# Second half of the key images transposed on TensorE instead of by DMA, with the order of the work searched anew

## The chip, the core and the metric

The kernel runs on one core of one Trainium2 chip. The metric is the device time of one execution in microseconds (us); the lower, the better. The profiles in this document each show one execution, and the times are medians of several executions.

## What is computed

Two kinds of layer alternate, twice each, over x of 2048 tokens by 512 features: x = x + A(layernorm(x)), x = x + B(layernorm(x)), and the same again. The cut reference of A, with 32 heads of 128 features, 8 memory rows and segments of 32 tokens:

```python
for s in range(n_seg):                      # 64 segments, one after the other
    h = concatenate([mem, xs[s]])           # 8 memory rows + 32 tokens = 40 rows
    q, k, v = h @ Wq, h @ Wk, h @ Wv        # each [32 heads, 40, 128]
    p = softmax(where(mask, q @ k.T * scale, -1e9))
    o = (p @ v, all heads) @ Wo             # [40, 512]
    mem = o[:8]                             # the next segment needs this
    outs.append(o[8:])
```

B is linear attention without a mask: phi(q) times the sum of phi(k) v over all tokens, divided by phi(q) times the sum of phi(k), times wo. Inputs and output are bfloat16.

## The kernel before, in words

The 64 segments of an A layer depend on each other through the memory rows, so the kernel goes through 2 x 64 steps in sequence. In step s the stationary operand of TensorE is `hT`, the 32 columns (8 memory rows and the first 24 tokens of the segment) of the current block; the last 8 tokens of four segments make up a "left" block of their own, which is prepared ahead for a group G of four segments (`prepare`, `left_block`). A step consists of these parts, named here by their place in the plan:

- `k0`, `k1`, `q0`, `q1` (function `turned`): `project` multiplies the block by half of a weight matrix (b = 0 or 1). It does so in 16 matmuls (L794), each with 512 moving columns: four chunks of the features, and for each chunk one matmul on each of the array's four 32-column strips. The result is evacuated by ACT or DVE (L623 or L624) into an `img` buffer, 128 x 512 in bfloat16. This image has to be transposed in blocks before attention can use it. There are two ways, chosen by the argument `dma`: one DMA transpose issued from SP (L807) that writes `kT` or `qT` directly, or 16 matmuls against the identity (L816) into a PSUM tile and one more evacuation of 128 x 512.
- `v0`, `v1`: the same projection, evacuated without a transpose.
- `mem0`, `mem1` (`mem_attention`, one call for each half b): scores against the left keys (L943, 4 matmuls) and against `kT` (L937, 16 matmuls), exp on ACT (L954), weights on DVE (L964), column sums on TensorE (L970), ln and exp on ACT (L973, L975), weighted values on TensorE (L980, L983), and the product on DVE (L987).
- `out`: the output projection (L1085, 64 matmuls of 256 columns on 32-column strips), and two evacuations into `outW`.
- `next` (`next_mem`): the new memory rows are moved into place by small matmuls (L1110), then evacuated into the next `hT`. The projections of step s + 1 start from there.
- `x` (`x_attention`, L1019, L1015, L1051, L1055): attention of the 24 tokens, which only the next step's `out` needs. Left blocks, layernorms (`prep`, L765), residual rows and B's work for finished tiles (`bi`, `bo`, L1247, L1281, L1350, L1358) lie between these parts too.

Before the change both halves of the keys go by DMA in all steps but the first and the last of a layer (62 steps in each of two layers, so 248 DMA transposes); the queries always go over TensorE. The left blocks use DMA transposes too (232 of them, L807, L829, L875). All of them are issued by SP, in one queue.

The order of the work is not written by hand. Every operation is a node of a planner (`_Prog`). `schedule` assigns nodes to engines and fixes each engine's order when the program is built, with costs such as 0.17 us + 0.833 ns per element for ACT, and for a key's DMA transpose a time to landing of `TURN` + 0.2 = 2.0 us. Among ready nodes the highest priority goes first: minus (step x `PERIOD` + `OFFSET` of the place). `OFFSET` is a table of several hundred numbers, found by a search. `MODE_SLACK` says how much priority TensorE gives up to stay in the same mode ("col" for 32-column strips, "full" for the whole array), and `LOOK` how long TensorE may be left waiting for a more urgent node. The engines then execute these fixed orders with semaphore waits: an instruction that waits holds up all that stands behind it on its engine.

Of the kernel before, what the change touches and what calls it, by code (L numbers as in the profile page):

```python
# [16 lines left out]
HOP = 0.06  # L17
PE_SWITCH = 0.1
TURN = 1.8
MODE_SLACK = 192.230600  # L20

LOOK = 0.053000

PERIOD = 13.5
OFFSET = {
# [2 lines left out]
    "ld2": (0.00,),  # L28
    "ld3": (0.00,),
    "ld4": (0.00,),  # L30
    "startF": (-170.65,),
    "prepF": (-362.95, -276.40, -279.35, -312.25, -284.40, -217.25, -201.70, -91.90, -249.05, -348.60, -91.55),
    "left0F": (-416.25, -385.35, -190.40, -192.15, -191.50, -260.05, -185.05, -323.65, 49.05, -312.35, -318.60,
        -241.55, -302.65, -428.10),
    "left1F": (-193.15, -172.40, -166.05, 8.55, -258.70, 143.10, -33.70, -147.70, -290.10, -305.35, 95.80, -299.95,
        -122.50, -62.05),
    "leftv0F": (-428.45, -202.00, -272.00, -246.25, -281.55, 122.35, -299.95, -328.60, -403.90),
    "leftv1F": (-236.20, -263.35, -302.50, -297.40, -85.80, -45.90, 124.65, 2.20, -49.90),
    "leftsF": (-234.20, -375.85, -265.20, -250.15),
    "xlF": (-310.30,),  # L40
    "k0F": (-347.90, -327.85, -45.95, -130.00, -426.00, -164.90, -319.75),
    "k1F": (-399.90, -270.75, -170.05, -162.00, -401.55, -54.25, -374.20),
    "q0F": (-283.40, -269.55, -303.95, -408.95, -255.55, 69.25, -299.55),
    "q1F": (-204.75, -132.60, -288.35, -54.15, -258.85, -365.30, -182.50),
    "v0F": (-414.65, -223.40, -19.35, 81.75, -230.45),
    "v1F": (-401.65, -20.40, -368.15, -227.30, 51.20),
    "qlF": (-245.40, -114.85),
    "mem0F": (-317.25, -11.55, -397.30, -321.65, -320.25, -248.15, -253.70, -229.35, -133.00, -179.30),
    "mem1F": (-370.65, -140.65, -279.95, -318.75, -212.15, -221.80, -405.65, -341.75, -281.65, -211.10),
    "warm": (42.25,),  # L50
    "outF": (-402.35, -81.30, -402.15, -242.85, -347.15, -401.55, -307.80, -298.10, -276.25, -259.15),
    "nextF": (-375.70, -276.25, -244.45),
    "xF": (-98.95, -278.35, -377.95, -152.15, -135.25, 32.50, -346.60, -281.05, -333.80, -305.40, -12.30, -315.60,
        -254.25, -391.50, -398.50, -375.10, -142.10, -246.05, -334.30, -87.65, -255.15, -235.40, 13532.05),
    "k0": (-401.55, -410.00, -408.65, -395.35, -74.20, -387.80),
    "k1": (-391.95, -393.55, -385.95, -421.75, -30.10, -383.50),
    "q0": (-390.25, -317.80, -318.55, -319.05, -274.20, -209.45, -235.60),
    "q1": (-318.10, -268.15, -290.55, -290.35, -195.95, -199.55, -227.60),
    "v0": (48.50, -288.20, -280.75, -292.45, -407.80),
    "v1": (-129.55, -240.70, 55.90, -105.15, -237.95),  # L60
    "ql": (-280.90, -136.95),
    "mem0": (-26.85, -405.55, -408.25, -272.75, -279.50, -104.85, -278.45, -267.70, -46.10, -243.25),
    "mem1": (-310.50, -287.80, -241.60, -278.85, -365.10, -292.95, -265.00, -282.35, -102.40, -283.10),
    "out": (-25.50, -276.55, -294.25, -203.55, -206.65, -210.35, -252.50, -482.00, -293.65, -307.90),
    "next": (-255.55, -256.05, -278.85),
    "res": (236.50, -313.60, -391.85, -316.15, -318.45, -213.15, -208.95, -209.00, -293.25, 28.80, -279.90,
        -138.50, 15.90, -283.25, -219.80),
    "x": (-93.20, -38.25, -293.70, -268.95, -391.70, -282.75, -266.00, -265.05, -145.40, -288.95, -131.60, -62.40,
        -274.15, -533.80, -295.10, -243.65, -187.65, -24.75, -364.70, -413.90, -387.65, -216.80, -254.50),
    "prep": (1.35, -36.30, -223.35, -207.00, -267.90, -50.60, -49.25, -48.35, -273.10, -44.30, -306.65),  # L70
    "left0": (-48.30, -401.20, -399.80, -62.90, -46.25, 32.70, -54.85, -105.00, -281.40, -268.85, -253.85, -280.75,
        -398.85),
    "left1": (-203.20, -273.65, -253.00, -268.75, -275.85, -144.15, -240.85, -222.15, -62.15, -26.20, -324.35,
        -249.50, 164.80),
    "leftv0": (-197.90, -242.35, -154.55, -352.25, -27.40, -18.85, -389.90, -343.05),
    "leftv1": (-37.05, -37.20, -17.30, 77.70, -243.10, -422.10, -312.45, -147.50),
    "lefts": (-233.40, -231.20, -282.65, -281.10),
    "xl": (8.50,),
    "bi": (-193.05, -276.60, -31.20, -282.75, -309.65, -103.40, -411.75, -293.35, -60.50, -323.30, -306.25, -50.60,
        222.00, -26.45, -419.70, 153.25, -239.30, -268.60, -45.00, -406.05, 10.80, 235.95, -34.25, -253.30,  # L80
        -258.15, -283.80, -225.85, -253.40, -289.90, -455.50, -380.70, -330.00),
    "k0L": (-397.65, -321.00, -290.45, -295.10, -149.00, -211.05, -209.60),
    "k1L": (-315.55, -249.05, -284.25, -222.90, -300.80, -226.80, -358.55),
    "lr": (-281.60, -387.40, -223.70, -194.55, -163.65, -294.00, -403.80, -281.80, -54.95, -32.55, -208.50,
        -309.95, -290.45),
    "xL": (-216.70, -398.20, -62.05, -12.50, -5.65, -146.85, -275.80, -37.65, 42.50, -160.75, -241.30, -2.50,
        -431.00, -191.10, -201.00, -409.30, -21.65, -235.10, -274.75, 30.60, -86.15),
    "outL": (-332.60, -340.75, -182.95, -373.55, -30.55, -381.10, -253.00, -312.90, -416.90, -25.90),
    "resL": (-28.25, -281.80),
    "biL": (-252.95, -263.60, -283.55, -413.10, -366.90, -266.00, -247.00, -280.95, -270.35, -405.60, -300.70,  # L90
        136.55, -156.95, -222.15, -94.65, 144.10, -155.20, -300.55, -274.15, -80.30, -106.30, -268.10, -202.50,
        -72.35, -256.40, -293.85, -84.10, -275.70, -178.05, -227.25, 24.00, -302.35),
    "bm": (-260.20, -231.30, -199.90, -417.75, -164.00, -416.45, -315.35, -149.90, -246.65, -188.85, -306.65,
        -193.85, -304.25),
    "boF": (-243.70, -216.35, -419.65, -205.95, -58.65, -230.20, -354.85, -261.35, -168.20, -314.80, -202.35),
    "bo": (-261.70, -389.05, -8.40, -226.30, -208.05, -365.20, 89.15, -317.00, -313.75, -60.60, -263.60),
    "ldL": (-267.05, -251.65),
    "boL": (-188.90, -322.50, -307.65, -221.35, -371.35, -300.60, -211.05, -102.75, -186.05, -221.05),
    "boZ": (-261.45, -73.35, -318.25, -222.40, -39.10, -170.70, -12.60, -83.90, -205.70, -19.35),
}  # L100


# [404 lines left out]
def _build_kernel(nc, A_x, A_mem0, A_Wq, A_Wk, A_Wv, A_Wo, A_seg_len, B_wqkv, B_wo, out):  # L507
# [8 lines left out]
    NSEG = S // SEG  # L516
# [18 lines left out]
    Wk_sb = sb("Wk_sb", [128, 4, H * DH])  # L535
# [45 lines left out]
    kT = av(1024).rearrange("p (h j x) -> p h j x", h=8, j=4)  # L581
# [195 lines left out]
    def a_layer(base, first):  # L777
# [413 lines left out]
        for s in range(NSEG):  # L1191
            G, g = divmod(s, 4)
            r2 = s % 2
            blk = hT[:, G % 2, g, :, :]
            bk = [("hTm", G % 2, g), ("hTx", G % 2, g)]
            if g == 0 and G + 1 < NT:
                tokens(G + 1, s)
            for b in range(2):
                at(s, "k%d" % b)
                turned(Wk_sb, "Wk", blk, bk, b, kT[:, 4 * b:4 * b + 4, :, :], ("kT", b), True, 0 < s < NSEG - 1)  # L1200
            for b in range(2):
                at(s, "q%d" % b)
                turned(Wq_sb, "Wq", blk, bk, b, qT[:, 4 * b:4 * b + 4, :, 0:32], ("qT", b), True, False)
            for b in range(2):
                at(s, "v%d" % b)
                tl = project(Wv_sb, "Wv", blk, bk, b, True)
                evac(vimg[:, r2, 512 * b:512 * b + 512], lambda tl=tl: tl.f32()[:, :], 512, tiles=[tl],
                     writes=[("v", r2, b)], urgent=True)
            for b in range(2):
                mem_attention(s, b)  # L1210
            if first and s == 0:
                warm(0, 14, [n for n in P.nodes if n.key == (0, "mem1F", 1)])
            w_of[s] = out_block(s)
            if s + 1 < NSEG:
                next_mem(s, w_of[s][0])
            if s > 0:
                residual((s - 1) // 4, (s - 1) % 4, w_of[s])
                if g == 0:
                    b_in(base + s + 2, G - 1, not first)
            x_attention(s)  # L1220
            if g == 2 and G + 1 < NT:
                prepare(G + 1, s)
# [197 lines left out]
```

## Time and profile before

| what | value |
|---|---|
| time, median of 3 runs | 1782.08 us (1778.4 to 1785.93) |
| profiled execution, its own time | 1783.98 us |
| span of the profiled execution | 1781.8 us |
| mean granted TensorE clock | 0.991 |
| PE matmul busy | 1656.4 us (93%) |
| PE weight load busy | 1063.9 us (60%) |
| DVE busy | 1062.1 us (60%) |
| ACT busy | 1172.9 us (66%) |
| POOL busy | 326.5 us (18%) |
| DMA transposes issued by SP | 480 |

"Busy" of PE counts a matmul from its start to its modelled end, and matmuls overlap, so it is not the share of PE's peak. "Idle before" and the waits name the instruction whose end released an engine. In the chain of waits, the run is followed back from its last instruction to what released each step.

### The profile page before, as it was taken

Reading aid. Unit: us, or ns where it says so; the run is one execution under the profiler, and the core shown is the slowest. Engines: PE = TensorE matmul, PEld = TensorE weight load, DVE = VectorE, ACT = ScalarE, POOL = GpSimd, SP = SyncE. Lnnn points to the kernel's source line nnn. Section 1 sums busy time; section 2 is a strip of 40 time slices with the busy share of each in tenths; the row PEclk is TensorE's granted clock in tenths of the full one; section 3 lists DMA queues with packets and bytes.
Section 4 is the critical chain, followed back from the end, with each engine's and each line's share of the span. In section 5 each row is a group of like instructions: output and inputs, shape, how many; then the busy total and the mean of one; then the engine's idle time right before and its main releaser. Section 6 shows DMA issues by size and latency. Waiting matters only on the chain.

```text
span 1781.8 us, 96722 instructions
## 1 busy us (share of the span) xinstructions
PE 1656.4 (93%) x43964; PEld 1063.9 (60%) x44043; DVE 1062.1 (60%) x3788; ACT 1172.9 (66%) x3117; POOL 326.5 (18%) x660
## 2 busy tenths in 40 slices
PE   5999999999999999999799999999999999999996
PEld 2656656665666665566456566666666656666563
DVE  3456666665666566565555666666665656665656
ACT  3666666666666666666466677767766766676665
POOL 2011211112121111222102111122221112221120
PEclk9999999999999999999899999999999999999998
DMA  9323323323233332332012333233333333332323
GB/s 378 79 48 53 56 54 51 61 49 56 53 53 57 51 61 44 57 56 50 25 33 42 59 56 60 50 56 59 53 62 56 54 54 54 56 59 53 62 76 99
DMA packets 295978, 113.46 MB, mean 64 GB/s; under 512 B 274552, under 2 KB 289712, under 8 KB 294032
## 3 DMA queue, kind: packets, MB, share of 16 engines
q1 hardware_dynamic: 272240, 74.91, 23.8%
q0 software_dynamic: 21744, 19.78, 5.3%
q10 hardware_dynamic: 1584, 12.58, 1.7%
q8 instruction: 344, 5.64, 1.4%
q14 instruction: 66, 0.54, 0.1%
HBM read 29.63 MB, written 10.49 MB: 23 GB/s over the span
## 4 chain that ended last, share of the span: by engine, by line
PE 62%; DMA 21%; DVE 9%; ACT 5%; issue 2%; POOL 1%; ACTq 0%; DVEq 0%
PE pb L794 31%; DMA arena_sb<-arena_sb 14%; PE pb L1085 11%; PE pb L1247 3%; PE pb L1051 3%; DVE arena_sb L624 3%; DMA dx_sb<-y_sb 2%; DMA arena_sb<-pq_scratch 2%; PE pb L816 2%; PE pb L970 2%; PE pb L937 2%; ACT arena_sb L623 1%; DMA Wk_sb<-in_A_Wk_dram 1%; DMA pq_scratch<-arena_sb 1%; PE pb L1110 1%
## 5 line engine op out<-in xcount | busy, mean ns | idle before, releaser
L623 ACT ACTIVATE arena_sb<-pb 128x512 bf16<-128x512 f32 (+6 forms) x1433 | 710.0, 500 | 295.7 <-PE pb L794 186.9
L639 POOL DMA_DIRECT2D dx_sb<-y_sb x504 | 253.7, 509 | 1126.1 <-DVE arena_sb L624 659.8
L794 PE MATMUL pb<-Wv_sb,arena_sb 128*32 128x512 bf16 x5120 | 357.3, 378 | 2.8 <-issue 2.8
L794 PE MATMUL pb<-Wk_sb,arena_sb 128*32 128x512 bf16 x5120 | 344.5, 383 | 5.0 <-DMA Wk_sb<-in_A_Wk_dram 4.2
L794 PE MATMUL pb<-Wq_sb,arena_sb 128*32 128x512 bf16 x5120 | 345.8, 381 | 0.9 <-DMA Wq_sb<-in_A_Wq_dram 0.6
L1085 PE MATMUL pb<-Wo_sb,arena_sb 128*32 128x256 bf16 x10368 | 335.1, 273 | 7.6 <-DVE arena_sb L987 5.9
L624 DVE COPY arena_sb<-arena_sb 128x128 bf16<-128x128 bf16 (+2 forms) x973 | 207.6, 213 | 148.2 <-DMA arena_sb<-arena_sb 92.6
L1085 PEld LDWEIGHTS pb<-Wo_sb,arena_sb 128*32 128x32 bf16 x10368 | 261.0, 97 | 47.2 <-DVE arena_sb L987 13.7
L624 DVE COPY arena_sb<-pb 128x512 bf16<-128x512 bf16 (+2 forms) x311 | 117.9, 381 | 192.3 <-PE pb L816 171.5
L624 DVE CAST arena_sb<-pb 128x512 bf16<-128x512 f32 (+3 forms) x388 | 186.7, 488 | 43.5 <-PE pb L794 29.5
L794 PEld LDWEIGHTS pb<-Wk_sb,arena_sb 128*32 128x32 bf16 x5120 | 127.6, 97 | 130.7 <-DVE arena_sb L624 18.8
L794 PEld LDWEIGHTS pb<-Wq_sb,arena_sb 128*32 128x32 bf16 x5120 | 134.9, 97 | 114.6 <-issue 2.1
L794 PEld LDWEIGHTS pb<-Wv_sb,arena_sb 128*32 128x32 bf16 x5120 | 113.2, 95 | 59.3 <-issue 4.3
L623 ACT ACTIVATE outW_sb<-pb 128x128 fp32r<-128x128 f32 x290 | 80.5, 278 | 100.8 <-PE pb L1085 90.2
L954 ACT ACTIVATE arena_sb<-pb 128x192 bf16<-128x192 f32 (+1 forms) x256 | 84.1, 328 | 86.1 <-PE pb L937 84.2
L964 DVE TENSOR_TENSOR arena_sb<-arena_sb 128x128 bf16<-128x128 bf16 x504 | 90.6, 221 | 25.9 <-ACT arena_sb L954 22.2
L816 PEld LDWEIGHTS pb<-id_sb,arena_sb 128*32 128x32 bf16 x4320 | 81.6, 97 | 32.0 <-ACT arena_sb L623 1.5
L1051 PE MATMUL pb<-arena_sb 128*128 128x128 bf16 x1024 | 98.5, 220 | 1.8 <-ACT arena_sb L623 0.7
L816 PE MATMUL pb<-id_sb,arena_sb 128*32 128x128 bf16 x4320 | 96.8, 219 | 0.7 <-ACT arena_sb L623 0.7
L987 DVE TENSOR_TENSOR arena_sb<-pb,arena_sb 128x128 bf16<-128x128 f32 x252 | 68.9, 288 | 43.4 <-ACT arena_sb L975 32.3
L937 PE MATMUL pb<-arena_sb 128*32 128x40 bf16 x4096 | 69.2, 180 | 27.2 <-DMA arena_sb<-arena_sb 26.7
L1121 DVE TENSOR_TENSOR y_sb<-pb,outW_sb 64x256 bf16<-64x256 f32 x158 | 65.7, 416 | 41.9 <-ACT outW_sb L623 37.8
(122 smaller groups left out, 1964.5 us busy)
## 6 DMA issues: line engine op xcount, KB each, us to landing
arena_sb<-arena_sb SPq DMA_TRANSPOSE x480, 2.8
Wq_sb<-in_A_Wq_dram ACTq DMA_DIRECT2D x1, 4096.0 KB, 13.8
Wk_sb<-in_A_Wk_dram ACTq DMA_DIRECT2D x1, 4096.0 KB, 24.7
Wv_sb<-in_A_Wv_dram ACTq DMA_DIRECT2D x1, 4096.0 KB, 35.1
Wo_sb<-in_A_Wo_dram SPq DMA_DIRECT2D x4, 1024.0 KB, 11.7
xs_scratch<-x_sb POOLq DMA_DIRECT2D x32, 128.0 KB, 2.1
pq_scratch<-arena_sb POOLq DMA_DIRECT2D x32, 128.0 KB, 2.3
dx_sb<-y_sb POOLq DMA_DIRECT2D x252, 12.0 KB, 2.0
```

Source lines behind the costliest of these rows:

```text
L623: return e.activation(o() if callable(o) else o, i() if callable(i) else i, ACTF.Copy)
L624: return e.tensor_copy(o() if callable(o) else o, i() if callable(i) else i)
L639: add(eng, lambda e: e.dma_start(o, i), 0.55 if eng == "pool" else 0.4, reads=reads, writes=writes, dsem="%s%d" % (kind, k), lat=lat + (0. ...
L794: r = pe.matmul(tl.f32()[32 * j:32 * j + 32, 0:512], blk[:, c, :], W[:, c, o:o + 512], start=(c == 0), stop=(c == 3), tile_position=(0, 32 ...
L816: r = pe.transpose(tt.bf16()[32 * j:32 * j + 32, 128 * i:128 * i + 128], img[:, k, o:o + 32], id_sb[:, :], tile_position=(0, 32 * j))
L937: r = pe.matmul(tl.f32()[32 * j:32 * j + 32, 40 * i:40 * i + 40], kT[:, hh, j, :], qT[:, hh, j, :], start=True, stop=True, tile_position=( ...
L954: add("act", lambda a: a.activation(PQ[:, r2, b, 0:nq], tl.f32()[:, 0:nq], ACTF.Exp, scale=SCALE), c_act(nq), tiles=[tl], writes=[("PQ", r ...
L964: add("dve", lambda v, a=a, p_=p_, w_=w_: v.tensor_tensor(wide(Pm[:, k, a, :]), p_.unsqueeze(2).to_broadcast([128, 4, 4, 8]), w_, ALU.mult ...
L987: add("dve", lambda v: v.tensor_tensor(oTb[:, s % NO, 16 * b:16 * b + 16, 0:8], pv.f32()[:, 0:128].rearrange("p (n q) -> p n q", q=8), Rm[ ...
L1051: r = pe.matmul(o, vimg[:, r2, e], Pbx[:, hh, :, :], start=i == 0, stop=False, skip_group_check=True)
L1085: r = pe.matmul(tl.f32()[32 * j:32 * j + 32, 0:256], oT[:, 4 * hh + n, :], Wo_sb[:, 8 * n + hh, 256 * d:256 * d + 256], start=(hh == 0 and ...
L1121: add("dve", lambda v: v.tensor_tensor(y_sb[0:64, k, :], tl.f32()[0:64, 0:256], outW[64:128, w, :].bitcast(F32), ALU.add), c_dve(256), rea ...
```

## The change

In the steps where both halves of the keys went by DMA, only half b = 0 still does; half b = 1 is transposed on TensorE, by the code that serves the queries. In addition `MODE_SLACK`, `LOOK` and the whole table `OFFSET` are replaced, so the order of the instructions on all engines is another one. The functions are otherwise the same.

```diff
-MODE_SLACK = 192.230600
+MODE_SLACK = 257.520800
-LOOK = 0.053000
+LOOK = 0.037900
 OFFSET = {
...
-    "k1": (-391.95, -393.55, -385.95, -421.75, -30.10, -383.50),
+    "k1": (-365.35, -358.40, -356.75, -359.10, -107.85, -297.25, -150.20),
...
             for b in range(2):
                 at(s, "k%d" % b)
-                turned(Wk_sb, "Wk", blk, bk, b, kT[:, 4 * b:4 * b + 4, :, :], ("kT", b), True, 0 < s < NSEG - 1)
+                turned(Wk_sb, "Wk", blk, bk, b, kT[:, 4 * b:4 * b + 4, :, :], ("kT", b), True, b == 0 and 0 < s < NSEG - 1)
```

The two lines of `OFFSET` stand for the whole table: all its numbers change but those of the first loads.

## The prediction

> **What bounds the kernel now.** I read the page first, for the shares of the engines and the chain of waits.
>
> ```profile
> PE 1656.4 (93%) x43964; PEld 1063.9 (60%) x44043; DVE 1062.1 (60%) x3788; ACT 1172.9 (66%) x3117; POOL 326.5 (18%) x660
> ...
> PE 62%; DMA 21%; DVE 9%; ACT 5%; issue 2%; POOL 1%; ACTq 0%; DVEq 0%
> PE pb L794 31%; DMA arena_sb<-arena_sb 14%; PE pb L1085 11%; PE pb L1247 3%; PE pb L1051 3%; DVE arena_sb L624 3%; DMA dx_sb<-y_sb 2%; DMA arena_sb<-pq_scratch 2%; PE pb L816 2%; PE pb L970 2%; PE pb L937 2%; ACT arena_sb L623 1%; DMA Wk_sb<-in_A_Wk_dram 1%; DMA pq_scratch<-arena_sb 1%; PE pb L1110 1%
> ```
>
> PE matters most, and transposing DMAs (arena_sb to arena_sb) hold 14% of the chain. The waits say who stands still for them, and the view of line L807 how long such a DMA takes:
>
> ```profile
> PEld pb L937 <- DMA arena_sb<-arena_sb: 43.3, 52, 1.6
> PE pb L937 <- DMA arena_sb<-arena_sb: 26.7, 40, 1.4
> DMA to landing us min/median/max: 2.4/2.7/5.4
> ```
>
> The scores (L937) wait for `kT`: 26.7 us of idle PE in 40 waits, the longest 1.4 us (the three numbers of a row). The landing is mostly near 2.7 us, at worst 5.4. The planner allows 2.0 us to landing after each issue, the same every time, so its order has no room for the late ones. The timeline of PE shows one of the late ones, and the chain in order of time the price of the other way:
>
> ```profile
> 932.77 0.83 PE L794 MATMUL pb<-Wv_sb,arena_sb 128*32 128x512 bf16 x12
> 934.67 0.28 PE L937 MATMUL pb<-arena_sb 128*32 128x40 bf16 x16 [1.07 <-DMA arena_sb<-arena_sb]
> ```
>
> ```profile
> 944.88 0.22 PE pb L816 x16
> ```
>
> In the first, the L937 of half 1 starts 1.90 us after twelve matmuls that need 0.65 us, so PE lost 1.25 us (1.07 by the row, which lets the last matmul end later). In the second, a transpose by 16 matmuls took 0.22 us of PE.
>
> A busy share of 93% hides overlap, so I counted PE anew from the starts of its matmuls in the trace. Four strips with 512 columns start every 215.7 ns, with 256 columns every 109 ns, with 128 every 56 ns; a full-array matmul of 128 columns takes 56 ns. All instructions of PE at such prices give 1531 us. The rest of the span is:
> - changes between 32-column strips and the full array: 604 in PE's order. After L1055 another full-array matmul follows in 55 ns, L794 in 147 to 182 ns; the median cost over the changes without a stall is 104 ns, so 604 x 0.104 = 63 us;
> - start and end, about 40 us (26 us lost in the first 45, 16 in the last 45);
> - stalls in the steps between, 135 us. By what stands still: L937 of half 1 27.8 (31 steps over 0.2 us), L937 and L943 of half 0 13.2, scores of left blocks (L894) 5.9, L1350 (a DMA from pq_scratch) 8.5, and the chain of the memory rows 58: L970 12.3, L980 11.5, L1085 12.7, L1110 17.0, first K projection 4.3. The rest is small pieces.
>
> Against the landing of its own DMA, half 0 had 1.17 us to spare in the median and stood at the landing in 11 of 124 steps; half 1 had 0.48 us and stood in 40. So PE has two costs, work and waits for late transposes, and the change exchanges one for the other.
>
> **What the Trainium skill says.** "TensorE: Matmul & The Clock Gate", Part 4: PE-mode transpose, says that the result of a transpose goes to PSUM and has to be copied from there, and gives about 275 ns for a 128x128 one in a kernel. The trace agrees on the copy (L624 after L816); one matmul of L816 lasts 219 ns on average, but 16 on four strips occupy PE for only 0.22 us. Part 3 of the same page (what overlaps and what doesn't) says that matmuls run strictly in order, so PE can't fill a wait for `kT` with later work; the row at 934.67 us agrees: L794 of a value projection was ready and started only after L937. "TensorEngine Tiling (Array Packing)", Key Properties, says that changing the tiling mode drains the engine; the 104 ns above are that price here. "Trainium Kernel Development and Optimization", Performance Expectations, warns that matmul busy time misleads, as they are pipelined: 1656 us busy against 1531 us of slots.
>
> **The change part by part.** The profiled execution took 1784.0 us, 1.9 above the median of 1782.1. Counts after the change are those of its order of instructions on each engine.
>
> 1. *Added on PE:* 124 x 16 matmuls of L816 (4320 become 6304), 124 x 0.223 us = +27.7 us. PE has no free engine beside it: all of it is on the path unless a stall shrinks.
> 2. *Mode changes:* 604 become 520, so 84 x 0.104 = -8.7 us. The transposes run on strips like their neighbours and add none.
> 3. *Removed waits:* half 1 of L937 no longer waits for a DMA, -27.8 us. What is late next is the copy out of PSUM. In the new order 1.09 us of PE work (median) stand between projection and transpose, where copying takes about 0.9 (0.60 on ACT and hand-offs of 0.3), and 1.54 us between transpose and L937, where the copy takes 0.7 to 0.9 (0.42 on DVE). The queries already live with 1.1 to 1.5 us ahead of their transposes, and none of these stalls. I leave 1 us: -26.8.
> 4. *Left blocks:* SP has 124 issues of 1.26 us less (480 transposes become 356), and left transposes no longer queue behind half 1. The new order also gives L894 more cover. I take -4.9 of 5.9 us.
> 5. *Half 0 remains on DMA:* the work between its projection and L937 shrinks from 4.57 to 4.36 us in the median, and without the second transpose behind it the landing may be a little sooner. Bounds -3 and +10 us; I take +3.
> 6. *The chain of the memory rows:* half 1 needs 2.98 us from projection to scores, not 4.29, so work moves behind it: cover from L970 to L980 of half 1 goes from 0.16 to 0.70 us, L1085 to L1110 from 0.83 to 0.86. But in 31 steps nothing at all stands between L1110 and the next K projection (at least 0.43 us before), and about 0.5 us is missing there: up to +15 us, while L1110 itself can lose about 10 and L970 with L980 about 11. Net -6; bounds -20 and +10.
> 7. *Copies:* 124 more of 128x512. By the order ACT has 56 more and DVE 68: 56 x 0.60 = 34 us and 68 x 0.42 = 29 us, partly offset by other copies that change engine. That is 2% of each, at 66% and 60%. It lies beside PE, except where another copy that PE waits for stands behind it. Nothing in the trace bounds this directly: from 0 (all in gaps) to 124 x 0.2 = 25 us (half a copy each step). I take +5.
> 8. *POOL and SP:* the row moves and transposes stand in a new order too, but they issue the same transfers as before (POOL 660 instructions in both), and POOL idles over 1100 us ahead of its dx_sb moves. I take 0; with the cover gone, a late row move costs its own 2 us, some ten times: the end of the kernel has one already.
>
> Sum: 1784.0 + 27.7 - 8.7 - 26.8 - 4.9 + 3 - 6 + 5 = 1773.3, or 1771 to 1772 against the median. **1772 us.**
>
> **The rivals.**
> - *A new wait for copies (slower).* The transpose of half 1 puts two more hand-offs into PE's strict order. If ACT or DVE has another copy ahead in 124 steps, PE stalls at the transpose or at L937 where it stood before at the landing. At 0.2 us per step this costs 25 us in place of the 6 in terms 3 and 7: 1772 + 19 = 1791; with 0.25 us and no gain in term 6, 1772 + 25 + 6 = 1803. I say 1797. It decides from about 0.15 us per step. For it: ACT is at 66% and has 512-wide copies in rows of up to five. Against: the queries' transposes have the same form and cover and hardly stall.
> - *The wait moves (even).* Half 0 stands at its landing in more steps, as half 1 no longer covers for it, and the hole between L1110 and the projection costs its 15 us: terms 5 and 6 at +8 and 0, so 1772 + 5 + 6 = 1783. For it: the chain is a recurrence, and less cover is left at both places.
> - *The shorter chain is worth more.* Terms 6 and 5 at -17 and 0: 1772 - 11 - 3 = 1758. For it: stalls in the chain are 58 us, and the lateness that begins at L937 of half 1 runs on into it.
> - *It does not do what it says:* excluded, the order has 1984 more matmuls and 124 fewer transposes.
>
> **How the numbers follow.** Forecast 0.44, copies 0.26, moved wait 0.20, longer gain 0.10. A measurement of this kernel can tell about 0.5%, 8.9 us, from no change: faster is below 1773.2, slower above 1791.0. The forecast's own range is 1763 to 1782, 0.25 of its 0.44 faster and 0.19 within; the moved wait gives 0.18 within and 0.02 slower; copies 0.26 slower; the longer gain 0.10 faster. So faster 0.35, same 0.37, slower 0.28. For 8 times in 10 the range goes from 1758, the longer gain, to 1800, which takes in most of the copies' case.
>
> **What would show it.** L816 should have 6304 matmuls at 0.22 us per 16; the waits of L937 for DMA should fall from 26.7 us to at most 15, all of half 0; the share of arena_sb transposes in the chain should fall from 14% to 9% or less; the mode changes should still cost about 104 ns. Wrong would be: idle PE at L816 or L937 behind L623 or L624 by over 10 us (copies), L937 for DMA still above 20 us or the first K projection behind its copy by over 15 us (moved wait), or stalls in the chain of memory rows down to 40 us (longer gain).

## The result, and the profile after

| what | before | after |
|---|---|---|
| time, median of 4 runs each | 1780.82 us (1778.4 to 1785.93) | 1760.54 us (1758.26 to 1762.2) |
| ratio, 95% interval | 1 | 0.9882 (0.9855 to 0.9908) |
| profiled execution, its span | 1783.98, 1781.8 us | 1759.18, 1757.0 us |
| mean granted TensorE clock | 0.991 | 0.993 |

The change gains 1.2%, 20 us by the medians and 24.8 us of span in the two profiled executions; the interval of the ratio stays clear of 1. The forecast was 1772. The changed code is one line shorter, so L794 is now L793, L937 is L936, and so on.

The busy times, the chain's shares, the costliest groups and the DMA issues on the page of the changed kernel:

```profile
PE 1671.6 (95%) x46027; PEld 1098.7 (63%) x46027; DVE 1133.8 (65%) x3960; ACT 1130.2 (64%) x3069; POOL 329.3 (19%) x660
...
PE 80%; DMA 8%; DVE 5%; ACT 5%; issue 1%; POOL 1%; ACTq 0%; DVEq 0%
PE pb L793 42%; PE pb L1084 14%; PE pb L815 4%; PE pb L1050 4%; DMA arena_sb<-arena_sb 4%; PE pb L1246 3%; DMA dx_sb<-y_sb 2%; PE pb L936 2%; DVE arena_sb L623 2%; PE pb L1280 2%; PE pb L969 1%; ACT arena_sb L622 1%; DMA Wk_sb<-in_A_Wk_dram 1%; PE pb L1109 1%; PE pb L764 1%
...
L815 PE MATMUL pb<-id_sb,arena_sb 128*32 128x128 bf16 x6304 | 135.7, 219 | 0.1
...
arena_sb<-arena_sb SPq DMA_TRANSPOSE x356, 2.8
```

The transposing DMAs fell from 14% of the chain to 4%, PE rose from 62% to 80%: the chain now runs through work of PE where it ran through landings. L815 has the 6304 matmuls that were counted. DVE rose by 72 us and ACT fell by 43: the new order also moved copies from ACT to DVE.

The waits of the scores for a DMA, in the list of waits (total us, times, longest; PEld is the weight load ahead of a matmul, PE the matmul itself):

```profile
PEld pb L936 <- DMA arena_sb<-arena_sb: 10.7, 20, 1.5
PE pb L936 <- DMA arena_sb<-arena_sb: 6.4, 12, 1.2
```

Before, these were 43.3 in 52 waits and 26.7 in 40. The timeline of PE in the changed kernel shows what is left (start, duration, instruction, idle before):

```profile
453.71 0.20 PE L942 MATMUL pb<-arena_sb 128*32 128x32 bf16 x4
454.41 0.28 PE L936 MATMUL pb<-arena_sb 128*32 128x40 bf16 x16 [0.50 <-DMA arena_sb<-arena_sb]
454.53 0.60 PE L793 MATMUL pb<-Wv_sb,arena_sb 128*32 128x512 bf16 x8
454.96 0.19 PE L942 MATMUL pb<-arena_sb 128*32 128x32 bf16 x4
454.99 0.27 PE L936 MATMUL pb<-arena_sb 128*32 128x40 bf16 x16
```

The first L936 is half 0, 0.50 us late behind its landing. The second is half 1, whose keys came over PE: it starts 0.03 us after its L942, with no wait.

The prediction's count of PE from the starts of its matmuls, made for both profiled executions (slots are the time that the matmuls need from start to start, stalls what stands between them beyond that; a mode change at 0.104 us, those seen in the records; its cost is taken off a stall, which makes the chain 55.7 us here and not the 58 of the prediction):

| us of the span | before | after | difference |
|---|---|---|---|
| matmul slots | 1531.1 | 1558.8 | +27.7 |
| mode changes (586, 506 seen) | 60.9 | 52.6 | -8.3 |
| L937 of half 1 | 27.8 | 0.4 | -27.4 |
| L937 and L943 of half 0 | 13.2 | 16.1 | +2.9 |
| left scores L894 | 5.9 | 0.1 | -5.8 |
| L1350, a DMA from pq_scratch | 8.5 | 1.8 | -6.7 |
| chain: L970, L980, L1085, L1110 | 52.2 | 22.8 | -29.4 |
| chain: first K projection | 3.5 | 16.7 | +13.2 |
| transposes of the queries | 0 | 2.6 | +2.6 |
| attention's product L1051 | 5.2 | 7.1 | +1.9 |
| other stalls in the steps | 10.6 | 17.2 | +6.6 |
| start, end, remainder to the span | 62.9 | 60.8 | -2.1 |

The table says that the 28 us of new PE work use up the 27 us of vanished waits, and that the gain is made elsewhere: in the chain of the memory rows (-16.2), in mode changes (-8.3), at L1350 and L894. The experiments ask whether these belong to the transpose, to the order, or to each other.

### The profile page after: what moved, and what is told of

It reads as the page before. It is cut to its first block, busy times and chain, and to the rows that moved or that the text cites. A ratio compares the mean times of both kernels' runs of the same rounds, so it can differ in the third digit from the quotient of the medians.

```text
span 1757.0 us, 101000 instructions
## 1 busy us (share of the span) xinstructions
PE 1671.6 (95%) x46027; PEld 1098.7 (63%) x46027; DVE 1133.8 (65%) x3960; ACT 1130.2 (64%) x3069; POOL 329.3 (19%) x660
## 4 chain that ended last, share of the span: by engine, by line
PE 80%; DMA 8%; DVE 5%; ACT 5%; issue 1%; POOL 1%; ACTq 0%; DVEq 0%
PE pb L793 42%; PE pb L1084 14%; PE pb L815 4%; PE pb L1050 4%; DMA arena_sb<-arena_sb 4%; PE pb L1246 3%; DMA dx_sb<-y_sb 2%; PE pb L936 2%; DVE arena_sb L623 2%; PE pb L1280 2%; PE pb L969 1%; ACT arena_sb L622 1%; DMA Wk_sb<-in_A_Wk_dram 1%; PE pb L1109 1%; PE pb L764 1%
## 5 line engine op out<-in xcount | busy, mean ns | idle before, releaser
L622 ACT ACTIVATE arena_sb<-pb 128x512 bf16<-128x512 f32 (+6 forms) x1375 | 674.3, 509 | 302.6 <-PE pb L793 223.4
L793 PE MATMUL pb<-Wk_sb,arena_sb 128*32 128x512 bf16 x5120 | 346.7, 382 | 16.5 <-DVE arena_sb L623 6.5
L793 PE MATMUL pb<-Wv_sb,arena_sb 128*32 128x512 bf16 x5120 | 354.0, 379 | 1.7 <-issue 1.6
L793 PE MATMUL pb<-Wq_sb,arena_sb 128*32 128x512 bf16 x5120 | 340.0, 381 | 0.5 <-DMA Wq_sb<-in_A_Wq_dram 0.5
L1084 PE MATMUL pb<-Wo_sb,arena_sb 128*32 128x256 bf16 x10368 | 329.5, 273 | 9.9 <-DVE arena_sb L986 8.8
L1084 PEld LDWEIGHTS pb<-Wo_sb,arena_sb 128*32 128x32 bf16 x10368 | 265.8, 97 | 42.4 <-DVE arena_sb L986 20.3
L623 DVE CAST arena_sb<-pb 128x512 bf16<-128x512 f32 (+3 forms) x459 | 232.7, 519 | 83.8 <-PE pb L793 66.0
L623 DVE COPY arena_sb<-pb 128x512 bf16<-128x512 bf16 (+2 forms) x422 | 150.5, 365 | 172.7 <-PE pb L815 156.9
L623 DVE COPY arena_sb<-arena_sb 32x256 bf16<-32x256 bf16 (+2 forms) x960 | 202.3, 211 | 72.4 <-PE pb L942 18.8
L793 PEld LDWEIGHTS pb<-Wk_sb,arena_sb 128*32 128x32 bf16 x5120 | 131.9, 97 | 122.0 <-DVE arena_sb L623 8.9
L793 PEld LDWEIGHTS pb<-Wq_sb,arena_sb 128*32 128x32 bf16 x5120 | 131.9, 97 | 116.5 <-issue 2.1
L793 PEld LDWEIGHTS pb<-Wv_sb,arena_sb 128*32 128x32 bf16 x5120 | 115.7, 95 | 48.4 <-issue 2.6
L815 PEld LDWEIGHTS pb<-id_sb,arena_sb 128*32 128x32 bf16 x6304 | 110.5, 97 | 53.6 <-DVE arena_sb L623 12.1
L815 PE MATMUL pb<-id_sb,arena_sb 128*32 128x128 bf16 x6304 | 135.7, 219 | 0.1
L1050 PE MATMUL pb<-arena_sb 128*128 128x128 bf16 x1024 | 114.0, 220 | 5.5 <-DVE arena_sb L623 4.2
L1050 PEld LDWEIGHTS pb<-arena_sb 128*128 128x128 bf16 x1024 | 69.4, 97 | 40.8 <-issue 19.3
## 6 DMA issues: line engine op xcount, KB each, us to landing
Wo_sb<-in_A_Wo_dram SPq DMA_DIRECT2D x4, 1024.0 KB, 11.7
```

Of the source, the lines that this page charges most:

```text
L622: return e.activation(o() if callable(o) else o, i() if callable(i) else i, ACTF.Copy)
L623: return e.tensor_copy(o() if callable(o) else o, i() if callable(i) else i)
L793: r = pe.matmul(tl.f32()[32 * j:32 * j + 32, 0:512], blk[:, c, :], W[:, c, o:o + 512], start=(c == 0), stop=(c == 3), tile_position=(0, 32 ...
L815: r = pe.transpose(tt.bf16()[32 * j:32 * j + 32, 128 * i:128 * i + 128], img[:, k, o:o + 32], id_sb[:, :], tile_position=(0, 32 * j))
L1050: r = pe.matmul(o, vimg[:, r2, e], Pbx[:, hh, :, :], start=i == 0, stop=False, skip_group_check=True)
L1084: r = pe.matmul(tl.f32()[32 * j:32 * j + 32, 0:256], oT[:, 4 * hh + n, :], Wo_sb[:, 8 * n + hh, 256 * d:256 * d + 256], start=(hh == 0 and ...
```

## The experiments

Each ratio is against the kernel before, run beside the variant; its medians there were 1774.3 us (the first four variants), 1776.6 (the changed kernel again and the three variants beside it) and 1779.6 (two later ones: the identity as half 0's keys, and the hole filled). Two versions that did not run beside each other are compared by their ratios.

### The code alone, the order's table alone

The changed code with the old `OFFSET`, `MODE_SLACK` and `LOOK` (the places that are new in `k1` take the values of `q1`):

```diff
-    "k1": (-391.95, -393.55, -385.95, -421.75, -30.10, -383.50),
+    "k1": (-391.95, -393.55, -385.95, -421.75, -195.95, -199.55, -227.60),
...
-                turned(Wk_sb, "Wk", blk, bk, b, kT[:, 4 * b:4 * b + 4, :, :], ("kT", b), True, 0 < s < NSEG - 1)
+                turned(Wk_sb, "Wk", blk, bk, b, kT[:, 4 * b:4 * b + 4, :, :], ("kT", b), True, b == 0 and 0 < s < NSEG - 1)
```

> Half 1 of the keys on TensorE as in the changed kernel, but with the table of priorities, MODE_SLACK and LOOK of the kernel before (the two new places of k1 take the values of q1). The count of its order gives 852 mode changes instead of 604, so PE has 27.7 us of transposes and 248 x 0.104 = 26 us of changes more than before. Theory 1 (the transposes pay only in an order made for them): the waits of half 1 (27) and of the left blocks (5) go, 1781 + 54 - 32 = about 1803 us. Rival (the gain is the transposes alone, whatever the order): 1770 us or less.

And the new table with both halves by DMA:

```diff
-    "k1": (-365.35, -358.40, -356.75, -359.10, -107.85, -297.25, -150.20),
+    "k1": (-365.35, -358.40, -356.75, -359.10, -107.85, -419.80),
...
-                turned(Wk_sb, "Wk", blk, bk, b, kT[:, 4 * b:4 * b + 4, :, :], ("kT", b), True, b == 0 and 0 < s < NSEG - 1)
+                turned(Wk_sb, "Wk", blk, bk, b, kT[:, 4 * b:4 * b + 4, :, :], ("kT", b), True, 0 < s < NSEG - 1)
```

> Both halves by DMA as before, with the table, MODE_SLACK and LOOK of the changed kernel. The count gives 682 mode changes (78 more, 8 us), cover of half 1 ahead of its scores 4.2 us as before, and no PE work between the last L1110 and the next K projection in 52 steps. Theory 1 (the removed wait makes the gain): the wait of L937 of half 1 is still there, 25 to 35 us, and with the holes of this order the time is 1790 to 1810 us. Rival (the new order alone makes the gain): 1765 us or less.

The first took 1949.9 us, ratio 1.0986 (1.0954 to 1.1018), the second 1968.7 us, ratio 1.110 (1.1064 to 1.1136; mean granted clocks 0.983 and 0.965, below the 0.99 of the kernel before; what that costs is not separated). Both theories missed both, by over 140 us. The waits of the first, in the list for the weight loads, and of the second:

```profile
PEld pb L1085 <- DVE arena_sb L987: 58.7, 82, 1.3
PEld pb L970 <- DVE arena_sb L964: 41.9, 67, 1.7
```

```profile
PEld pb L1084 <- DVE arena_sb L986: 118.1, 106, 2.9
PEld pb L936 <- DMA arena_sb<-arena_sb: 44.7, 59, 2.6
```

In both, PE stands in the chain of the memory rows (L1085, L970; L1084 in the second), and in the second the scores (L936) still wait for the landings as before: by the count, stalls of 235 and 303 us in the steps in place of 127. The priorities were found for another set of operations; which of them misled the planner I did not trace. Neither part alone holds the gain, and each of the two tables tried here is worth something only with the code that it was searched for. That also makes these two a poor way to split the change; all later kernels but the last keep an order as it is and change what the operations do.

### The price of PE's work: each transpose twice

The changed kernel in its own order, with the 16 matmuls of each half-1 transpose issued twice (half 1 goes over PE in all 64 steps of both layers, so 128 times):

```diff
+            twice = dkey == ("kT", 1)
             def tr(pe):
-                for i in range(4):
+                for i in 2 * list(range(4)) if twice else range(4):
```

> The changed kernel in its order, but PE does each transpose of half 1 twice into the same PSUM tile (32 matmuls instead of 16; the planner is told the old cost, so that the order is the same). Theory 1 (PE's strict order is the bound, added PE work costs its own time): 27.7 us more, less a few us of the wait of half 0 that it covers, 1784 to 1788 us. Rival (the chain of the memory rows is the bound and PE has room): 1761 to 1770 us.

1789.4 us, ratio 1.0096 (1.0069 to 1.0123). Against 0.9888, the mean of the changed kernel's two ratios (the second is shown below), that is 0.0208 x 1774.3 = +37 us, with some 6 us of uncertainty; the spans of the two profiles differ by 29.5. Of the 29.5, slots are 28.5, half 0 waits 6 less for its landing (10.1), and start and end are 5.8 more, which I can't explain. PE's work costs its full time, with little idle time that takes it in: the rival, that PE has room, falls.

### The old order without half 1's wait

The kernel before with its own order and all its work, except that in the steps the scores of half 1 read the keys of half 0, and wait for that DMA; half 1's transposes are still issued, but nothing on PE waits for them:

```diff
-                        r = pe.matmul(tl.f32()[32 * j:32 * j + 32, 40 * i:40 * i + 40], kT[:, hh, j, :],
+                        r = pe.matmul(tl.f32()[32 * j:32 * j + 32, 40 * i:40 * i + 40], kT[:, hh % 4 if 0 < s < NSEG - 2 else hh, j, :],
...
     P.schedule()
...
+    for nd in P.committed:
+        if nd.key is not None and nd.key[1] == "mem1" and nd.key[2] == 1 and (nd.key[0] + 1, "k0") in turn:
+            nd.sync.discard(turn[nd.key[0], "k1"])
+            nd.sync.add(turn[nd.key[0], "k0"])
+            turn[nd.key[0] + 1, "k0"].sync.add(nd)
```

> The kernel before in its own order, but in the steps 1 to 61 of each layer the scores of half 1 read half 0 of the keys' image, and wait for that one instead of their own DMA, which still runs. This changes part of the computation: half of the heads use keys of other heads. No PE work is added. Theory 1a (the wait costs its own time, and the rest of the gain in the chain is the new order's): 27 us less than before, about 1754 us, with 55 us of stalls left at L970, L980, L1085, L1110 and the K projection. Theory 1b (lateness of half 1 also makes those stalls): 16 us less still, about 1738 us. Rival (the chain takes the gain back, since the wait moves to the next link): 1770 to 1781 us.

1752.8 us, ratio 0.9879 (0.9854 to 0.9904): -21.5 us, 17 to 26 by the interval, a little under the 27 of theory 1a and far from the 43 of 1b. (The profiles' spans differ by 29.7, but that of the kernel before was not taken beside this one.) The list of waits of this kernel, and its views of lines L1110 and L970 with the idle time before them, weight loads and matmuls together (us, times):

```profile
PE pb L937 <- DMA arena_sb<-arena_sb: 5.3, 12, 1.2
```

```profile
  ACT outW_sb L623: 38.6, 99
  DVE arena_sb L964: 35.9, 123
```

The first was 26.7 in 40 waits. The other two are what decides: in the kernel before the same rows of L1110 and L970 read

```profile
  ACT outW_sb L623: 38.8, 100
  DVE arena_sb L964: 32.5, 113
```

and in the changed kernel (now L1109 and L969)

```profile
  ACT outW_sb L622: 10.8, 26
  DVE arena_sb L963: 17.6, 43
```

By the count, the stall of half 1 went (27.8 to 0.4) and the five stalls of the chain stayed: 56.9 against 55.7. So the chain did not stand still because half 1 was late; lateness at L937 doesn't run on into it, and both rivals fall, the chain that shrinks along with the wait and the chain that takes the gain back. What is left for the -16.2 us in the chain is the new order. The kernel with doubled transposes supports it: the new order with 28.5 us more PE work at half 1 has the same row of L1110 as the changed kernel, 10.7 in 26. Which feature of the order does it, less time from half 1's projection to its scores or other work between the chain's members, is not shown, nor does any run have the new order's gain without the transposes.

This kernel can't be told from the changed one in time (0.9879 against 0.9882 and 0.9894): the old order without half 1's wait gains as much as the whole change. By the count, the transposes on PE remove the wait and cost as much as it did, and what the change gains comes with the order.

### The price of a copy

The changed kernel, run again beside three variants of it:

> The changed kernel as it is, beside the runs of this call, so that their times have it on the same chip: by its first runs 0.986 to 0.991 of the time before.

1757.7 us, ratio 0.9894 (0.987 to 0.9918), span 1755.4. In the first variant, the second copy of half 1 is preceded by another of the same size, from the same PSUM tile into its own `img` buffer, 86 on ACT and 42 on DVE:

```diff
+            if dkey == ("kT", 1):
+                fn, spare = once.fn, copy(img[:, k, :], lambda: tt.bf16()[:, 0:512])
+
+                def both(e):
+                    spare(e)
+                    return fn(e)
+                once.fn = both
...
```

> The changed kernel in its order, but the copy of half 1 out of PSUM is preceded by a copy of the same size into the image's own buffer, which nobody reads again: 0.42 us more on DVE or 0.60 us on ACT in each step, and half 1 is later by that. Theory (the copies lie beside PE; 1.5 us of PE work stand between transpose and scores and one copy needs 0.7 to 0.9): 0 to 10 us more than the changed kernel. Rival (copies are what PE waits for next): half of each copy or more shows, 25 to 65 us more.

1770.1 us, ratio 0.996 (0.9943 to 0.9977), +12.3 us against the changed kernel beside it, with some 5 us of uncertainty. The copies added are about 86 x 0.60 + 42 x 0.42 = 69 us, so 18% of them show. (The busy time of ACT and DVE grew by 44 us only, as two copies in a row overlap; of that it is 28%.) The waits of the scores against left keys (L954 in this kernel, L942 in the changed one) for the evacuations:

```profile
PEld pb L954 <- DVE arena_sb L623: 23.1, 76, 2.0
PEld pb L954 <- ACT arena_sb L622: 13.8, 26, 0.9
```

```profile
PEld pb L942 <- DVE arena_sb L623: 20.5, 71, 1.4
PEld pb L942 <- ACT arena_sb L622: 5.4, 25, 0.3
```

The waits behind both grew, the one behind ACT most. These scores read the queries and not half 1's keys, so the likely way is that the queries' copies stand behind half 1's on the same engine; that was not traced further. The copies are hidden for the most part, but not free: the expected 0 to 10 can't be excluded, the 25 to 65 of the other theory can.

### What half 0's landing still costs

In the second variant the scores of half 0 read the keys of half 1, which PE made, and wait for their copy:

```diff
-                        r = pe.matmul(tl.f32()[32 * j:32 * j + 32, 40 * i:40 * i + 40], kT[:, hh, j, :],
+                        r = pe.matmul(tl.f32()[32 * j:32 * j + 32, 40 * i:40 * i + 40],
+                                      kT[:, hh + 4 if b == 0 and 0 < s < NSEG - 2 else hh, j, :],
...
+            main.sync.discard(turn)
+            main.sync.add(copy1)
```

> The changed kernel in its order, but in the steps 1 to 61 of each layer the scores of half 0 read the image of half 1, which TensorE made, and wait for that instead of half 0's DMA, which still runs. This changes part of the computation: half of the heads use keys of other heads. Theory (the DMA of half 0 costs what PE stands before its scores, 16 us by the trace, of which part is the left scores' wait for queries): 8 to 16 us less than the changed kernel, so that taking half 0 to TensorE as well (27.7 us of work for it) would lose 12 to 20. Rival (that DMA costs more than its stalls show, through the chain): 25 us less or more.

1761.8 us, ratio 0.9918 (0.9893 to 0.9943): 4 us over the changed kernel beside it, which is within the noise of the two, where 8 to 16 of gain were expected. Its list of waits shows why this tells nothing of the DMA:

```profile
PEld pb L936 <- ACT arena_sb L622: 14.2, 56, 0.7
```

Half 1's copy is not earlier than half 0's landing; one wait was exchanged for the other. So a later kernel gives half 0's scores a key that is always there, the identity's first 32 columns, and drops their wait for the DMA (which is still issued):

```diff
-                        r = pe.matmul(tl.f32()[32 * j:32 * j + 32, 40 * i:40 * i + 40], kT[:, hh, j, :],
+                        w = id_sb[:, 0:32] if b == 0 and 0 < s < NSEG - 2 else kT[:, hh, j, :]
+                        r = pe.matmul(tl.f32()[32 * j:32 * j + 32, 40 * i:40 * i + 40], w,
...
+            at[s, "mem0", 1].sync.remove(at[s, "k0", 5])
```

> The changed kernel in its order, but in the steps 1 to 61 of each layer the scores of half 0 use columns of the identity in place of the keys' image, so that they wait for no DMA and no copy of keys (the DMA still runs). This changes part of the computation: half of the heads have no keys. Theory (half 0's DMA costs the stalls ahead of L937 of half 0): 6 to 14 us less than the changed kernel; taking half 0 to TensorE as well, at 27.7 us of work, would then lose 14 to 22. Rival (that DMA costs more than its stalls show): 25 us less or more, and both halves on TensorE would pay.

1748.0 us, ratio 0.9827 (0.9808 to 0.9846). At 0.9888 the changed kernel would take 1759.7 beside it: -11.7 us, as the theory expected. The chain of waits of this kernel has DMA at 4%, from 8%:

```profile
PE 85%; ACT 5%; DVE 4%; DMA 4%; issue 1%; POOL 0%; ACTq 0%; DVEq 0%
```

Putting half 0 on PE as well would add another 27.7 us of slots to win at most these 12, unless an order found for it wins more. That is argued from two measured prices; it wasn't run.

### The price of a mode change

In the third variant one full-array matmul of 8 columns, into unused columns of the transpose's own tile, stands before each half-1 transpose. This makes two more mode changes in each of the 128 steps, 256 in all (the expectation counted 124 steps):

```diff
             def tr(pe):
+                if dkey == ("kT", 1):
+                    pe.matmul(tt.f32()[:, 256:264], id_sb[:, :], id_sb[:, 0:8], start=True, stop=True)
```

> The changed kernel in its order, with one more full-array matmul of 8 columns (25 ns) ahead of each transpose of half 1, into columns that nobody reads: two mode changes more per step. Theory (a change costs 0.104 us of PE): 124 x (2 x 0.104 + 0.025) = 29 us more than the changed kernel, less up to 5 that covers half 0's DMA. Rival (the drain hides in the pipeline when so little is in flight, and the 0.104 us come from what follows a change by chance): under 10 us more.

1781.0 us, ratio 1.0024 (1.0012 to 1.0035), +23.2 us against the changed kernel beside it. The timeline of PE in this kernel:

```profile
443.09 0.40 PE L817 MATMUL pb<-id_sb,arena_sb 128*32 128x128 bf16 x16
443.42 0.18 PE L813 MATMUL pb<-id_sb 128*128 128x8 bf16 x1
443.52 0.41 PE L817 MATMUL pb<-id_sb,arena_sb 128*32 128x128 bf16 x16
```

The single L813 starts 0.33 us after the 16 transposes before it, which fill 0.22, and the next transposes start 0.10 after it. Over all 128 places the starts give 28.1 us; without 128 matmuls at 0.025 that is 24.9 / 256 = 0.097 us for a change. Shorter waits, of half 0 above all, gave back some 5. The 0.104 us read off the trace of before are about right, and the rival of under 10 us falls.

### The hole before the K projection

In 18 steps the changed order puts four of attention's products (L1051, L1055) directly ahead of L1110 on PE, and nothing between L1110 and the next K projection. Here they stand behind it:

```diff
+        held = pe[nxt - 4:nxt]
+        if [nd.key for nd in held] != [(s, "x", k) for k in (17, 18, 19, 20)]:
+            continue
+        pe[nxt - 4:nxt + 2] = pe[nxt:nxt + 2] + held
...
```

> The changed kernel with one edit to PE's order: in the 18 steps of the first layer, and at its edges, in which nothing stands between the last L1110 and the next K projection and x_attention's products stand ahead of it, the second four of these products (L1051, L1055, 0.28 us) are moved to that place. No work is added; the mode changes per step go up by two. Theory (the hole costs 0.5 us per step, and L1110 could start 0.3 us sooner): 0.1 to 0.3 us in each of 18 steps, 2 to 6 us less than the changed kernel. Rival (the copy into hT is late on its own engine, behind other work): no difference.

1756.9 us, ratio 0.9874 (0.9855 to 0.9893): not to be told from 0.9882 and 0.9894. In the count the stall of the K projection fell from 16.7 to 7.8 us, L1110 rose by 1.4, mode changes by 3.8 and half 0 lost 2.6 of its wait; the span is 1754.0, 1.4 and 3.0 below the two of the changed kernel. This hole was worth less than its width, since the work that fills it leaves another place. It is the one variant meant to beat the changed kernel, and no gain over it is shown.

## Why the prediction was right, and where it was off

The forecast, 1772, had the sign right and the size not: it lay 11.5 us over the time, and the gain, 20 us by the medians, was twice the forecast's 10. The time is inside the wide range (1758 to 1800) but near its lower end, and below the forecast's own range (1763 to 1782). By the prediction's own limits it came out faster, to which it had given 0.35, a little less than to same. Its parts before the change add to 1531 + 63 + 40 + 135 = 1769 us and leave 13 us of the 1781.8 us span in no part; the table above has what no part holds in its last row, which changed by 2.1 only. Step by step, forecast and measured:

1. *Added on PE*: +27.7, and +27.7 in the count, which is the same number of matmuls at the same price; that such work is paid in full is what the doubled transposes show.
2. *Mode changes*: -8.7, measured -8.3 of those recorded; the price was confirmed from the side at 0.097.
3. *Half 1's wait*: -26.8, measured -27.4; taken out of the old order, the wait gave this stall in the count and left the chain's, and 17 to 26 us of time.
4. *Left blocks*: -4.9, measured -5.8.
5. *Half 0*: +3, measured +2.9. One sentence of the prediction on it is wrong: the planner's 2.0 us to landing come on top of the issue, for which it counts about 1.25 us more, while the 2.4/2.7/5.4 us of the profile begin with the issue. So its order has room for the median landing, and lacks it only for the late ones.
6. *The chain of the memory rows*: -6, measured -16.2 (55.7 to 39.5). **This is the mis-sized term.** Its parts were named rightly: the K projection lost 13.2, of at most 15; L1110 gained 12.1, of about 10; L970 and L980 gained 15.0, of about 11; L1085 gained 2.3. The net of -6 was these parts in full, +15 - 10 - 11; in the count the gains are 29.4 in place of 21, of which 4.0 more at L970 and L980, 2.1 at L1110 and 2.3 at L1085, which had nothing, and the loss is 1.8 less. At L970 and L980 the median cover grew by 0.54 us in one place, and what it gave was 0.12 us per step over both, so the median of the cover was no measure of it.
7. *Copies*: +5, measured +11 in small pieces (queries 2.6, L1051 1.9, the rest 6.6), if all of that is put down to copies; the spare copy's 18% would give 124 more copies (63 us) about 11 as well. If so, the term was too low by half. Its picture of 2% more on each engine did not come: ACT is busy 43 us less and DVE 72 more, since other copies went from ACT to DVE.
8. *POOL and SP*: 0, and in the sum nothing was there for L1350, a wait for a DMA that POOL issues. It went from 8.5 to 1.8 us, and to 1.0 in the second run of the changed kernel. No experiment isolates why: the variant in the old order has 5.8, those in the new one 1.5 to 3.6, which points to the order.

The terms off are -10.2 (6), +6 (7) and -6.7 (L1350); with start and end at -2.1, they make up 13.0 of the 14.1 us between the forecast's -10.7 and the -24.8 of the profiled pair. The error of the copies has the opposite sign of the others and hid part of them, which is luck. The rival of the longer gain had the size of term 6 (-17), its time (1758) and its sign (stalls in the chain down to 40, measured 39.5), but its reason, that lateness from L937 runs on into the chain, fell with the old order that lost only this wait. Its other reason, that the chain had 58 us of stalls to win from, holds. The rival of the copies did not come about: PE stalls at the transposes of half 1 for 0 us and at L937 of half 1 for 0.4. That of the moved wait came about in part: the timeline of PE shows the hole, here with L793 0.34 us late behind the copy of `hT`,

```profile
407.25 0.32 PE L1109 MATMUL pb<-selm_sb,outW_sb 128*32 128x16 f32 x16
407.67 0.39 DVE L623 CAST arena_sb<-pb 128x32 bf16<-128x32 f32 x2
407.92 1.26 PE L793 MATMUL pb<-Wk_sb,arena_sb 128*32 128x512 bf16 x20 [0.34 <-DVE arena_sb L623]
```

and its sum of 16.7 us is over the 15 set for it, but L1110 gave back nearly as much.

## What to carry to other kernels

Where one engine with a strict order sets the time, count its slots, its mode changes and its stalls from the starts of its instructions: the exchange of a wait for work could be priced here to about a microsecond of the count. What an order searched anew does to the waits of a recurrent chain could not: summed place by place from median covers, it came to a third of what was measured (-6 for -16.2). Such a term needs a wide range, or the stalls step by step. To split a change of work and order, keep the order and change what its operations do: half of such a change with the other half's order measures only the mismatch.

## What the runs showed of the hardware

- A change between 32-column strips and the full array costs PE about 0.1 us: 0.104 in the median of the changes recorded, 0.097 by the experiment that adds 256 of them.
- A transpose of 128x512 by 16 matmuls on four strips occupies PE for 0.223 us, though one of its matmuls lasts 219 ns; copies added beside it showed at 18% of their time. The landing of the DMA for a tile of the same size varies from 2.4 to 5.4 us after issue. The waits for the late ones cost the kernel before 28 us at half 1, in an order that is fixed when the program is built.
